# Starting the first block's FFN five slots later in a slot-scheduled attention and FFN kernel

## The chip, the core and the metric

The kernel runs on one core of a Trainium2 chip. The metric is device time in microseconds (us), the median of three runs. One execution is also profiled, and it has a time and a span of its own (first to last instruction).

The engines are named as in the profile: PE (TensorE matmuls; PEld its weight loads), DVE (VectorE), ACT (ScalarE), POOL (GpSimd) and SP (the queue that issues most DMAs). A trailing q (SPq) is an engine's sequencer.

## The reference

```python
# u, v: (4, 3136, 256), z: (4, 3136, 64)
scores = (1.0 / S) * np.matmul(z, z.transpose(0, 2, 1))
attn = np.maximum(scores, 0.0) ** 2
x = u * np.matmul(attn, v)
# w_in (256, 1024), conv_w (3, 1024), w_out (1024, 256)
h = np.maximum(x @ w_in, 0.0)
conv_out = sum(conv_w[k] * hp[:, k:k + S, :] for k in range(3))   # hp: h padded by one row
gate = 1.0 / (1.0 + np.exp(-conv_out))
return h * gate @ w_out
```

This is attention with squared ReLU in place of softmax, multiplied by `u`, and an FFN of 1024 channels whose gate is a three-tap convolution along the sequence. The FFN weights arrive as 64-bit floats.

## The kernel before

**Tiling.** Each batch's 3136 queries are cut into six blocks of 512 and a remainder of 64. There are 24 blocks (`NBLK`). A block goes over 25 key tiles (`NJ`) of 128 keys, one per *slot*, so there are 600 slots, numbered through; block 0 is slots 0 to 24. Products are made accurate by splitting each operand into a high and a low part, so that one product takes two or three matmuls. A slot's attention is eight matmuls of 512 columns: two for scores (`scores`, lines 409 and 410, into a PSUM bank named `s`, for the tile four slots ahead) and six for attention times values (`attend`, line 535, three into the accumulator `av0`, three into `av1`).

**Between scores and attention.** ACT takes the ReLU (line 489, `t<-s`), DVE squares it (line 504, `s<-s,t`), ACT makes the high part (line 513, `ah<-s`), DVE the low part (line 171, `al<-s,ah`). In later blocks some tiles come by a transposing DMA instead and ACT squares them.

**The joint of two blocks.** `av0` and `av1` are single buffers. When a block ends, `gate_x` multiplies its result by `u`: DVE reads `av0` (line 672, `ut<-av,ut`) and ACT reads `av1` (line 667, `x<-av`). Only then may PE write the next block's first product. Once per batch the remainder's product (line 617, 25 matmuls) comes first at the joint, and it writes `av0`.

**The FFN of a block** runs beside the attention of the next. `split_x` (class `xl<-ut,xh`, on DVE and POOL) makes its operands; its hidden channels are eight tiles, `f` 0 to 7. Tile f has six matmuls in (lines 705 to 708), then ACT, DVE (two taps at line 749, a product at line 763) and POOL (`gl<-hb,gh`), and ten and eleven slots later six matmuls out (lines 780 to 782), three in each slot. `FS` gives a tile's slot, counted from the start of the next block.

**The weights** are turned from 64-bit to two 32-bit parts in the kernel, in 16 *pieces* of 128x256, one per `f` for `w_in` and `w_out`. `WS` holds a piece's slot. A piece costs DVE two instructions (lines 316 and 320) in that slot and two (lines 328 and 333) in the next; ACT two, POOL two and ACT a copy. The intermediate values of the first pieces lie in PSUM (tile `wp`), by the limit `W_P = 22` on the slot or by the list `W_B`; those of the others in SBUF (tile `wr`). For the pieces in `W_A`, line 333 is replaced by ACT and POOL work.

**The order** is written out by hand: `at(slot, class, ...)` appends a call to a slot, the loop over `k` emits them class by class, and each engine works its instructions off in that order. In a slot, `PE0` calls (matmuls out) come before `attend`; scores and `PE1` calls (matmuls in) come after it. Below slot `K_O` odd slots' scores go to other PSUM banks than `s`, and ReLU and square are emitted before the splits.

Of the kernel before, what the change touches and what calls it, by code (L numbers as in the profile page):

```python
# [30 lines left out]
DG = [1, 8, 15, 22]  # L31


K_O = 35
Q0 = 3
C0 = [0, 1, 2, 3, 16, 17, 22, 23, 4, 5, 18, 19, 8, 9, 20, 21, 6, 7, 10, 11, 14, 15, 12, 13, 24]

FS = [2, 5, 8, 11, 15, 18, 21, 24]  # L40
RELU, TAP, ST1, ST2, SIG, GATE, GHI, OUT0, OUT1 = 1, 2, 2, 3, 4, 4, 5, 10, 11
EVAC = 12
UL = 18
XS = 1

C_GATE, C_ST1, C_ST2, C_G, C_SIG, C_HI = 0, 2, 2, 2, 1, 3
C_RELU, C_TAP, C_XS, C_EV, C_V = 3, 1, 3, 3, 5
# [2 lines left out]
WARM = 7  # L50
VO = 4
Z1 = -3
WS = [2, 6, 8, 12, 16, 19, 21, 25, 27, 33, 36, 38, 40, 41, 46, 52]
WST = [0, 1, 1, 2, 3]
W_E = ["GGGGGGGGGGGGGGGG", "AAAAAAAAAAAAAAAA"]
W_C = 7
W_A = [9, 14]
W_B = [6, 7]
SQ = [26, 46]
W_P = 22  # L60

# [18 lines left out]
def kernel(  # L80
# [21 lines left out]
    NJ = (S + P - 1) // P  # L102
# [5 lines left out]
    FC = DFF // P  # L108
# [288 lines left out]
    def scores(k):  # L397
# [3 lines left out]

        if k < K_O and k % 2:
            tag, n = ("ph", 2) if k < NJ else (f"o{k // 2 % 2}", 1)
# [415 lines left out]
    V, A, G = nc.vector, nc.scalar, nc.gpsimd  # L819
# [4 lines left out]
    PRE, MID, VEC, POST, PE0, PE1 = range(6)  # L824

    def at(slot, cls, fn, *args):
        ev[slot][cls].append((fn, args))
# [3 lines left out]
    for q in zs[2:]:  # L831
        s = min(C0.index(j) for j in range(q * CB, min(q * CB + CB, NJ))) - LA - 3
# [11 lines left out]
    for b in range(1, B):  # L844
        k0 = (b * QB - 1) * NJ
        for q in range(QB + 1):
            s = k0 - (QB - 2 - q) * NJ + (12 if q % 2 == 0 else 4)
            if q == QB - 2:
                s = k0 + 6
            elif q == QB - 1:  # L850
                s = k0 + NJ + 6
            elif q == QB:
                s = k0 + 9
            if b == 1 and q < 2:
                s = (Q0 - QB) * NJ + NJ + k0 + 4 + 8 * q
# [3 lines left out]
        for j in range(0, NJ, 2):  # L859
            s = k0 + max(last[j] + 2, last.get(j + 1, 0) + 2, V0 + V1 * j // NJ)  # L860
            if j == NJ - 1:
                s = k0 + V0 - 2
# [5 lines left out]
    for blk in range(1, NBLK):  # L868
        s = blk * NJ + E3
# [4 lines left out]
    for blk in range(PK, NBLK):  # L874
        s = blk * NJ + (R_E if blk % QB == RB else E24[blk % QB])
# [6 lines left out]
    for b in range(B):  # L882
# [9 lines left out]
        for i in range(n + 1):  # L892
            s = k5 + (R_J + 2 * i + R_L * (i == n - 1) // 2 if i < n else R_D + 1) + 1
# [14 lines left out]
    def prep_w_at(n, what, f, i, s):  # L908
        if not wps and W_P:
            wps["w"] = ps.tile([P, 2, D], F32, tag="o1", name="wp")  # L910
        bank = wps["w"] if s < W_P else None
        if i in W_B and not n:
            bank = ps.tile([P, 512], F32, tag="ph", name="wp", bufs=2).rearrange("p (a n) -> p a n", a=2)
        prep_w(n, what, f, *(E[x[i]] for x in W_E), bank, nc.gpsimd if i in W_A else None)

    need = [(NJ + FS[f], "in", f) for f in range(FC)] + [(NJ + FS[f] + OUT0, "out", f) for f in range(FC)]
    for i, (_, what, f) in enumerate(sorted(need)):
        s = WS[i]
        at(s - 4, POST, load_w, what, f)
# [2 lines left out]
    for n in range(4):  # L922
        at(W_C + n, POST, prep_conv, n)
    for blk in range(NBLK):
        at(blk * NJ + UL, POST, load_u, blk)

    def before_end(slot, *args):
        if slot < NS:
            at(slot, *args)

    for blk in range(NBLK - 1):
        k0 = (blk + 1) * NJ
        at(k0, C_GATE, gate_x, blk, G)
        at(k0 + XS, C_XS, split_x, blk, (V, G))
        for f in range(FC):
            s = k0 + FS[f]
            if s == NS - 1:
                break
            at(s, POST, ffn_halo, blk, f)
            at(s, PE1, ffn_in, blk, f)  # L940
            at(s + RELU, C_RELU, ffn_relu, blk, f)
            at(s + RELU, C_RELU, ffn_keep, blk, f)
            at(s + TAP, C_TAP, ffn_tap, blk, f)
            at(s + ST1, C_ST1, ffn_conv, blk, f, 1)
            at(s + ST2, C_ST2, ffn_conv, blk, f, 2)
            before_end(s + SIG, C_SIG, ffn_sig, blk, f)
            before_end(s + GATE, C_G, ffn_gate, blk, f, G)
            before_end(s + GHI, C_HI, ffn_hi, blk, f, A)
            before_end(s + GHI, PE1, ffn_lo, blk, f, G)
            before_end(s + OUT0, PE0, ffn_out, blk, f, 0)  # L950
            before_end(s + OUT1, PE0, ffn_out, blk, f, 1)
        if blk < NBLK - 2:
            at(s + EVAC, C_EV, evac, blk)
            at(s + EVAC + 2, POST, store, blk)
# [97 lines left out]
    def run(fns):  # L1052
        for fn, args in fns:
            fn(*args)

    with tc.manual_schedule():
# [15 lines left out]
        for k in range(-LA, NS):  # L1072
            e = ev[k]
            run(e[PRE])
            early = k + LT < K_O
            if early and 0 <= k + LT:
# [81 lines left out]
```

## Time and profile before

| | |
|---|---|
| runs | 1467.34, 1466.86, 1466.7; median 1466.86 us |
| profiled execution | 1467.12 us, of which the span is 1465.3 us |
| busy share of the span | PE 99%, PEld 86%, DVE 78%, ACT 80%, POOL 59% |
| granted TensorE clock | 1.00 of full speed over the span |
| DMA | 205.24 MB, mean 140 GB/s |

Matmul rows overlap: one of 512 columns is 0.38 us long, and in a full stretch the next begins 0.22 us after it. So the busy share of PE says little here; the number of matmuls in a stretch tells how full PE is. DVE's rows overlap in the same way by some 0.08 us.

### The profile page before, as it was taken

To read this page: it belongs to the slowest core of one execution; us is meant where nothing else is said; L and a number is where in the kernel's file an instruction comes from. 1 tells how busy PE (TensorE), PEld (TensorE's weight loads), DVE (VectorE), ACT (ScalarE), POOL (GpSimd) and SP (SyncE) were. 2 spreads that over 40 slices of the span, in tenths; PEclk is the share of its full clock that TensorE was granted. 3 is DMA by queue.
4 is the path that set the end of the run, shared out by engine and by line. 5 is a ranking of instruction groups with operands and counts; after the bars stand their busy time and mean duration, and the time that the engine had idled before them with its cause. 6 is when DMAs were issued, how large, how long until landed. Compare 5 with 4: busy or idle time off the path is not lost.

```text
span 1465.3 us, 22715 instructions
## 1 busy us (share of the span) xinstructions
PE 1451.6 (99%) x6781; PEld 1260.7 (86%) x6781; DVE 1143.4 (78%) x1776; ACT 1178.5 (80%) x2246; POOL 864.0 (59%) x1218
## 2 busy tenths in 40 slices
PE   9999999999999999999999999999999999999998
PEld 7778888888888888888888888888888888888887
DVE  8998777768787777767777877876778777787677
ACT  8878887878877877878888788787887777878767
POOL 7875656447866654545776654554586654554433
PEclk9999999999999999999999999999999999999999
DMA  6544666865445556678444555586644446567621
GB/s 198 164 132 104 153 142 156 169 150 138 147 134 142 135 132 157 138 149 178 133 149 132 138 140 134 140 172 138 157 149 137 132 122 150 129 132 168 133 63 37
DMA packets 432380, 205.24 MB, mean 140 GB/s; under 512 B 330753, under 2 KB 411905, under 8 KB 432257
## 3 DMA queue, kind: packets, MB, share of 16 engines
q1 hardware_dynamic: 431584, 203.40, 56.9%
q8 instruction: 53, 0.87, 0.3%
q14 instruction: 71, 0.57, 0.1%
q10 hardware_dynamic: 672, 0.40, 0.1%
HBM read 36.59 MB, written 86.90 MB: 84 GB/s over the span
## 4 chain that ended last, share of the span: by engine, by line
PE 87%; POOL 4%; ACT 3%; DVE 3%; issue 2%; DMA 0%; SPq 0%; ACTq 0%; POOLq 0%; DVEq 0%
PE av L535 46%; PE ph L708 5%; PE o L780 5%; PE o L782 5%; PE ph L705 5%; PE o L781 5%; PE ph L706 5%; PE s L409 4%; PE s L410 4%; PE av L617 1%; DVE ph L749 1%; POOL vv L171 1%; POOL pl L439 1%; ACT ph L744 1%; DVE al L171 1%
## 5 line engine op out<-in xcount | busy, mean ns | idle before, releaser
L535 PE MATMUL av<-ah,vv 128*128 128x512 f32 x2400 | 708.7, 379 | 1.4 <-ACT ah L513 0.7
L171 DVE TENSOR_TENSOR al<-s,ah 128x512 fp32r<-128x512 f32 x576 | 397.5, 690 | 225.4 <-PE av L535 116.8
L535 PEld LDWEIGHTS av<-ah,vv 128*128 128x128 f32 x2400 | 449.5, 189 | 64.9 <-ACT ah L513 1.1
L535 PE MATMUL av<-al,vv 128*128 128x512 f32 x1152 | 437.0, 379 | 0.4
L171 POOL TENSOR_TENSOR gl<-hb,gh 128x512 fp32r<-128x512 f32 x192 | 245.3, 1277 | 157.1 <-ACT gh L174 149.3
L749 DVE SCALAR_TENSOR_TENSOR ph<-hb,cw,ph 128x512 f32<-128x512 f32 x384 | 286.8, 747 | 9.4 <-ACT ph L744 9.0
L439 POOL COPY pl<-t 128x1024 uint16<-128x1024 uint16 (+1 forms) x257 | 260.9, 1017 | 2.2 <-DMA dq<-pl 1.1
L535 PEld LDWEIGHTS av<-al,vv 128*128 128x128 f32 x1152 | 217.7, 189 | 32.6 <-DVE al L171 1.8
L504 DVE TENSOR_TENSOR s<-s,t 128x512 f32<-128x512 f32 x275 | 191.8, 697 | 61.5 <-ACT t L489 60.8
L489 ACT ACTIVATE t<-s 128x512 f32<-128x512 f32 x277 | 166.1, 599 | 64.1 <-PE s L410 60.0
L513 ACT CAST ah<-s 128x512 fp32r<-128x512 f32 x277 | 163.3, 590 | 59.8 <-DVE s L504 59.5
L756 ACT ACTIVATE ph<-ph 128x512 f32<-128x512 f32 (+1 forms) x200 | 115.4, 577 | 78.1 <-DVE ph L749 74.7
L739 POOL COPY halo<-hb 128x2 f32<-128x2 f32 x160 | 31.1, 194 | 240.6 <-ACT hb L734 232.2
L484 ACT ACTIVATE s<-tp 128x512 f32<-128x512 f32 x278 | 165.3, 596 | 4.9 <-DMA tp<-dd 3.0
L705 PE MATMUL ph<-xh,wih 128*128 128x512 f32 x384 | 145.8, 380 | 1.1 <-DVE hb L763 1.1
L780 PE MATMUL o<-gh,wol 128*128 128x512 f32 x384 | 145.9, 380 | 0.0
L782 PE MATMUL o<-gl,woh 128*128 128x512 f32 x384 | 145.5, 379 | 0.0
L706 PE MATMUL ph<-xh,wil 128*128 128x512 f32 x384 | 145.5, 379 | 0.0
L781 PE MATMUL o<-gh,woh 128*128 128x512 f32 x384 | 145.5, 379 | 0.0
L744 ACT ACTIVATE ph<-hb,cw 128x512 f32<-128x512 f32 x192 | 133.7, 696 | 6.2 <-POOL halo L739 0.4
L763 DVE TENSOR_TENSOR hb<-ph,hb 128x512 f32<-128x512 f32 x192 | 131.8, 686 | 5.1 <-ACT ph L756 0.7
L734 ACT ACTIVATE hb<-ph 128x512 f32<-128x512 f32 x192 | 114.2, 595 | 17.7 <-PE ph L708 16.3
(138 smaller groups left out, 2091.3 us busy)
## 6 DMA issues: line engine op xcount, KB each, us to landing
dq<-pl SPq DMA_DIRECT2D x232, 256.0 KB, 2.7
st<-in_v_dram SPq DMA_DIRECT2D x48, 256.0 KB, 3.1
ut<-in_u_dram SPq DMA_DIRECT2D x24, 512.0 KB, 4.1
out_dram<-ob SPq DMA_DIRECT2D x19, 512.0 KB, 3.8
st<-in_z_dram SPq DMA_DIRECT2D x24, 256.0 KB, 3.2
sh<-sc SPq DMA_DIRECT2D x44, 128.0 KB, 2.4
dd<-pl SPq DMA_DIRECT2D x69, 64.0 KB, 2.2
dd<-pl SPq DMA_DIRECT2D x23, 192.0 KB, 2.4
```

The lines of the kernel that those rows point to most:

```text
L171: eng.tensor_tensor(out=out, in0=a, in1=b.bitcast(F32), op=ALU.subtract)
L439: nc.gpsimd.tensor_copy(pl[k], src.bitcast(U16).rearrange("p (n h) -> p h n", h=2))
L484: nc.scalar.activation(sc[k][:, :NB], tp[k], AF.Square, scale=SC1**-0.5)
L489: nc.scalar.activation(rl[k], sc[k][:, :NB], AF.Relu, scale=SC1)
L504: nc.vector.tensor_tensor(out=s, in0=s, in1=rl[k], op=ALU.mult)
L535: nc.tensor.matmul(o, lhsT=w[:, j, d], rhs=pairs(r), start=first and i == 0, stop=last and i == len(ops) - 1)
L705: nc.tensor.matmul(o, lhsT=wih[:, dc, w], rhs=pairs(xh[blk][:, dc]), start=(dc == 0), stop=False)
L706: nc.tensor.matmul(o, lhsT=wil[:, dc, w], rhs=pairs(xh[blk][:, dc]), start=False, stop=False)
L749: nc.vector.scalar_tensor_tensor(out=c, in0=hb[blk, f][:, k : e + k], scalar=cw[:, f, k : k + 1], in1=c, op0=ALU.mult, op1=ALU.add,)
L780: nc.tensor.matmul(o, lhsT=wol[:, f, d], rhs=pairs(h), start=(f == 0), stop=False)
L781: nc.tensor.matmul(o, lhsT=woh[:, f, d], rhs=pairs(h), start=False, stop=False)
L782: nc.tensor.matmul(o, lhsT=woh[:, f, d], rhs=pairs(l), start=False, stop=(f == FC - 1))
```

## The change

Block 0's FFN is moved by `LAG = 5` slots, block 1's by four, and so on to block 4's by one; from block 5 on nothing moves. The eight tiles of a moved block are three slots apart throughout (`FSL`), so each moved block takes 24 slots and not 25. `split_x`, `evac` (the copy out) and the store move with their block, and `load_u` of blocks 2 to 5 moves where its buffer would not be free. The loop that emits matmuls in and out is otherwise the same.

The sixteen pieces are put at slots 2 to 57 and no longer 2 to 52, three or four apart from slot 10 on, and piece 8 joins the pieces with intermediate values in PSUM. The limit `K_O` moves along by five.

```diff
-K_O = 35
+K_O = 40
 FS = [2, 5, 8, 11, 15, 18, 21, 24]
+FSL = [2, 5, 8, 11, 14, 17, 20, 23]
+LAG = 5
-WS = [2, 6, 8, 12, 16, 19, 21, 25, 27, 33, 36, 38, 40, 41, 46, 52]
+WS = [2, 6, 10, 13, 17, 20, 24, 28, 32, 36, 39, 43, 46, 49, 53, 57]
-W_B = [6, 7]
+W_B = [6, 7, 8]
...
+    def lag(blk):
+        return max(0, LAG - blk)
+
+    def ffn_slots(blk):
+        x = lag(blk)
+        return [(blk + 1) * NJ + x + s for s in (FSL if x else FS)]
...
-        at(blk * NJ + UL, POST, load_u, blk)
+        at(blk * NJ + max(UL, lag(blk - 2) + 15 if blk > 1 else 0), POST, load_u, blk)
...
-        at(k0 + XS, C_XS, split_x, blk, (V, G))
-        for f in range(FC):
-            s = k0 + FS[f]
+        at(k0 + XS + lag(blk), C_XS, split_x, blk, (V, G))
+        for f, s in enumerate(ffn_slots(blk)):
```

Line numbers of the changed kernel are higher by two up to the schedule and by eight in its loop. Three places are shown.

**DVE, slots 40 and 41.** `al` rows are one per slot; `wr` rows are pieces. Before:

```order
L171 TENSOR_TENSOR al<-s,ah 128x512
L504 TENSOR_TENSOR s<-s,t 128x512
L763 TENSOR_TENSOR hb<-ph,hb 128x512
L316 TENSOR_SCALAR wr<-wr 128x256
L320 TENSOR_SCALAR wr<-wr 128x256
L171 TENSOR_TENSOR al<-s,ah 128x512
L504 TENSOR_TENSOR s<-s,t 128x512
L328 SCALAR_TENSOR_TENSOR wr<-wr 128x256
L333 SCALAR_TENSOR_TENSOR wr<-wr 128x256
L316 TENSOR_SCALAR wr<-wr 128x256
L320 TENSOR_SCALAR wr<-wr 128x256
```

Changed, the same engine from slot 40 on:

```order
L173 TENSOR_TENSOR al<-s,ah 128x512
L506 TENSOR_TENSOR s<-s,t 128x512
L751 SCALAR_TENSOR_TENSOR ph<-hb,cw,ph 128x512
L330 SCALAR_TENSOR_TENSOR wr<-wr 128x256
L335 SCALAR_TENSOR_TENSOR wr<-wr 128x256
L173 TENSOR_TENSOR al<-s,ah 128x512
L506 TENSOR_TENSOR s<-s,t 128x512
L751 SCALAR_TENSOR_TENSOR ph<-hb,cw,ph 128x512
L173 TENSOR_TENSOR al<-s,ah 128x512
L506 TENSOR_TENSOR s<-s,t 128x512
L765 TENSOR_TENSOR hb<-ph,hb 128x512
```

Before, slots 40 and 41 hold six instructions of two pieces; changed, slots 40 to 42 hold the last two of one piece.

**PE, the joint at slot 50** (end of block 1's attention, `av` rows; the first `av` rows are slot 49, the last ones slot 50). Before:

```order
L535 MATMUL av_780<-ah,vv 128x512 x2
L535 MATMUL av_780<-al,vv 128x512
L409 MATMUL s<-zq,zh 128x512
L410 MATMUL s<-zq,zl 128x512
L705 MATMUL ph<-xh,wih 128x512
L706 MATMUL ph<-xh,wil 128x512
L705 MATMUL ph<-xh,wih 128x512
L706 MATMUL ph<-xh,wil 128x512
L708 MATMUL ph<-xl,wih 128x512 x2
L780 MATMUL o_1108<-gh,wol 128x512
L781 MATMUL o_1108<-gh,woh 128x512
L782 MATMUL o_1108<-gl,woh 128x512
```

Changed, from the same place to slot 50's attention:

```order
L537 MATMUL av_773<-ah,vv 128x512 x2
L537 MATMUL av_773<-al,vv 128x512
L411 MATMUL s<-zq,zh 128x512
L412 MATMUL s<-zq,zl 128x512
L537 MATMUL av_1467<-ah,vv 128x512 x2
L537 MATMUL av_1467<-al,vv 128x512
```

Eleven matmuls stood between the two blocks' products, and now two do.

**PE, the joint at slot 125** (end of batch 0's attention; `ar` is the remainder's operand, and its product writes the bank that `av_2891` or `av_2874` held). Before:

```order
L535 MATMUL av_2891<-al,vv 128x512
L535 MATMUL av_2892<-ah,vv 128x512 x2
L535 MATMUL av_2892<-al,vv 128x512
L705 MATMUL ph<-xh,wih 128x512
L706 MATMUL ph<-xh,wil 128x512
L705 MATMUL ph<-xh,wih 128x512
L706 MATMUL ph<-xh,wil 128x512
L708 MATMUL ph<-xl,wih 128x512 x2
L780 MATMUL o_3218<-gh,wol 128x512
L781 MATMUL o_3218<-gh,woh 128x512
L782 MATMUL o_3218<-gl,woh 128x512
L617 MATMUL av_3556<-vv,ar 128x512 x25
```

Changed:

```order
L782 MATMUL o_3259<-gh,wol 128x512
L783 MATMUL o_3259<-gh,woh 128x512
L784 MATMUL o_3259<-gl,woh 128x512
L537 MATMUL av_2874<-ah,vv 128x512 x2
L537 MATMUL av_2874<-al,vv 128x512
L537 MATMUL av_2875<-ah,vv 128x512 x2
L537 MATMUL av_2875<-al,vv 128x512
L619 MATMUL av_3543<-vv,ar 128x512 x25
L707 MATMUL ph<-xh,wih 128x512
```

Six matmuls in and three out stood between the last product and the remainder's; now three matmuls out stand ahead of slot 124's attention and the six in behind the remainder.

## Rows read from the trace of the kernel before

**Rows 1.** The page's first part: busy us of each engine (share of span).

```profile
PE 1451.6 (99%) x6781; PEld 1260.7 (86%) x6781; DVE 1143.4 (78%) x1776; ACT 1178.5 (80%) x2246; POOL 864.0 (59%) x1218
```

**Rows 2.** By stretch: length, busy PE, PEld, DVE, ACT, POOL (count); clock; DMA.

```profile
20.00:50.00 30.00, 29.77 (x136) 24.92 (x135) 29.03 (x59) 27.38 (x61) 28.90 (x36) 1.00 0.71 219
50.00:70.00 20.00, 18.55 (x82) 14.49 (x81) 18.80 (x34) 17.65 (x39) 14.69 (x22) 1.00 0.39 109
70.00:110.00 40.00, 37.24 (x165) 29.93 (x164) 37.42 (x63) 31.55 (x65) 31.06 (x42) 1.00 0.48 142
110.00:140.00 30.00, 30.00 (x141) 25.74 (x140) 25.82 (x44) 26.73 (x53) 18.61 (x28) 1.00 0.33 85
140.00:290.00 150.00, 150.00 (x705) 131.36 (x704) 116.23 (x176) 123.77 (x233) 83.50 (x118) 1.00 0.70 155
```

**Rows 3.** Waits of PE, 0 to 200 us: total us, times, longest.

```profile
PE s L409 <- DVE al L171: 2.5, 3, 1.6
...
PE av L535 <- ACT x L667: 0.6, 1, 0.6
PE ph L708 <- POOL xl L171: 0.5, 1, 0.5
```

**Rows 4.** PE's timeline at 89 us: start, length, [idle before, releaser].

```profile
88.82 0.38 PE L535 MATMUL av<-al,vv 128*128 128x512 f32 x1
90.85 0.51 PE L409 MATMUL s<-zq,zh 128*128 128x512 f32 x1 [1.65 <-DVE al L171]
```

**Rows 5.** DVE's groups by form, 10 to 140 us: count, busy, mean ns, idle before.

```profile
L328 DVE SCALAR_TENSOR_TENSOR wr<-wr 128x256 uint32<-128x256 uint32 x8 | 5.4, 671 | 0.0
L316 DVE TENSOR_SCALAR wr<-wr 128x256 uint32<-128x256 uint32 x8 | 4.6, 576 | 0.0
L320 DVE TENSOR_SCALAR wp<-wr 128x256 uint32<-128x256 uint32 x8 | 4.1, 514 | 0.3
L320 DVE TENSOR_SCALAR wr<-wr 128x256 uint32<-128x256 uint32 x8 | 3.9, 492 | 0.0
L333 DVE SCALAR_TENSOR_TENSOR wr<-wr,wp 128x256 f32<-128x256 uint32 x8 | 3.9, 482 | 0.0
L316 DVE TENSOR_SCALAR wp<-wr 128x256 uint32<-128x256 uint32 x8 | 3.8, 472 | 0.0
L328 DVE SCALAR_TENSOR_TENSOR wr<-wr,wp 128x256 uint32<-128x256 uint32 x8 | 3.7, 466 | 0.0
L333 DVE SCALAR_TENSOR_TENSOR wr<-wr 128x256 f32<-128x256 uint32 x6 | 3.5, 581 | 0.0
```

**Rows 6.** DVE's timeline, two pieces at 75 and 81 to 90 us.

```profile
75.00 0.31 DVE L320 TENSOR_SCALAR wr<-wr 128x256 uint32<-128x256 uint32 x1
...
80.53 0.69 DVE L171 TENSOR_TENSOR al<-s,ah 128x512 fp32r<-128x512 f32 x1
81.14 0.69 DVE L504 TENSOR_TENSOR s<-s,t 128x512 f32<-128x512 f32 x1
...
88.15 1.31 DVE L316 TENSOR_SCALAR wr<-wr 128x256 uint32<-128x256 uint32 x1
```

**Rows 7.** PE, ACT and DVE timelines at slot 50's joint.

```profile
116.77 0.38 PE L535 MATMUL av<-al,vv 128*128 128x512 f32 x1
117.25 0.60 ACT L667 ACTIVATE x<-av 128x512 f32<-128x512 f32 x1
118.22 0.68 DVE L672 SCALAR_TENSOR_TENSOR ut<-av,ut 128x512 f32<-128x512 f32 x1
```

**Rows 8.** PE and DVE timelines at slot 125's joint.

```profile
289.75 0.38 PE L410 MATMUL s<-zq,zl 128*128 128x512 f32 x1
291.04 0.38 PE L535 MATMUL av<-al,vv 128*128 128x512 f32 x1
292.30 0.69 DVE L672 SCALAR_TENSOR_TENSOR ut<-av,ut 128x512 f32<-128x512 f32 x1
293.20 5.56 PE L617 MATMUL av<-vv,ar 128*128 128x512 f32 x25
```

More of the change, by code (lines that the diff above doesn't have):

```diff
@@ L914, in prep_w_at @@
         prep_w(n, what, f, *(E[x[i]] for x in W_E), bank, nc.gpsimd if i in W_A else None)
-    need = [(NJ + FS[f], "in", f) for f in range(FC)] + [(NJ + FS[f] + OUT0, "out", f) for f in range(FC)]
+    def lag(blk):
[3 more added lines that the diff above has]
+        return [(blk + 1) * NJ + x + s for s in (FSL if x else FS)]
+    need = [(s + o, w, f) for w, o in (("in", 0), ("out", OUT0)) for f, s in enumerate(ffn_slots(0))]
     for i, (_, what, f) in enumerate(sorted(need)):
```

## The prediction

> **What bounds the kernel now.** I read the page's first part, then the stretches, then PE's waits, then the timelines where PE stands still. PE is busy for 99% of the span [rows 1], so there is little to gain anywhere; the question is where PE is *not* full. Since matmul rows overlap, I count them. From 140 to 290 us there are 705 in 150 us, 0.213 us each, and this I take as a full PE. By it 136 matmuls are worth 28.9 us in the 30 us from 20 to 50, 82 are worth 17.4 in the next 20, 165 are worth 35.1 in the 40 up to 110, and 141 are worth 30.0 in the 30 up to 140 [rows 2]. PE thus loses 1.1, 2.6 and 4.9 us, and then nothing: 8.6 us in all, before 110 us. That is the room that this change works in (0.6% of the span).
>
> In those 90 us DVE is busy for 29.03 + 18.80 + 37.42 = 85.3 us, 95%; where PE is full it is busy for 116.23 of 150, 77% [rows 2]. Most of the named waits of PE there end with DVE's low part (2.5 us) [rows 3], the longest at 88.82, where the next matmul begins only at 90.85 [rows 4]. So DVE limits this part. What it has there and not later are the sixteen weight pieces.
>
> **What a piece costs.** The four DVE instructions of a piece take 0.472 + 0.514 + 0.466 + 0.482 = 1.93 us with intermediates in PSUM, and 0.576 + 0.492 + 0.671 + 0.581 = 2.32 in SBUF [rows 5]. Neighbouring rows overlap: a row of 0.69 is followed after 0.61 [rows 6]. I take off 0.08 four times: 1.6 and 2.0 us.
>
> The SBUF form is dear because it is uneven: line 320 took 0.31 us at 75.00, and line 316, the same kind of instruction, 1.31 at 88.15 [rows 6], against means of 0.49 and 0.58 [rows 5]. The Trainium skill (SBUF — State Buffer, "Who interferes with whom") gives a rule for this: a `tensor_scalar` from SBUF to SBUF takes a port pair that it shares with GpSimd, and whichever comes second waits for the other's whole instruction; the trace agrees in so far as one SBUF form spans 0.31 to 1.31 us. By that rule a piece that meets no POOL instruction would cost about 1.25 us (0.31 + 0.31 + 0.47 + 0.48 less the overlap) and the balance below would have room; I stay with the mean, since POOL is busy there.
>
> **The spacing, before and changed.** How much DVE has to spare: in FFN blocks 23% of PE's time [rows 2]. A block has 25 x 8 + 8 x 12 = 296 matmuls, 63 us, so a slot lasts 2.5 us and leaves DVE 0.57. In block 0 a slot is eight matmuls, 1.7 us, and DVE has two instructions of 0.61 there [rows 6], so 0.5 is left.
>
> Before, slots 33 to 41 hold five pieces: 10 us against 9 x 0.57 = 5.1. The deficit of 4.9 is just what PE loses from 70 to 110 us. Slots 12 to 27 hold six pieces, 9.6, and the joint's gate and low part of x, 1.2 more, against 16 x 0.5 = 8; the deficit of 2.8 stands beside 2.6 measured from 50 to 70. So the sum of DVE's work explains both.
>
> Changed, slots 13 to 31 hold five pieces, 8.0, and 1.2 for the joint and x, against 19 x 0.5 = 9.5: no deficit. Slots 32 to 58 hold the last eight, one of them now in PSUM: 1.6 + 7 x 2.0 = 15.6 against 27 x 0.57 = 15.4: balanced. Losses are then due to unevenness alone. The bounds: 0, as from 110 to 140 us, where two pieces lie in 30 us [rows 2], and what is lost now. The even spacing puts me near the lower bound, but the balance has nothing to spare: I take 0.3 of 1.1, 1.1 of 2.6 (0.5 of it the wait for POOL's `xl` [rows 3], which moves along with `split_x`, one slot ahead of the matmuls as before), and 1.2 of 4.9. **The stretch gives back 0.8 + 1.5 + 3.7 = 6.0 us**, between 1 and 8.6.
>
> **What the change adds: joints without cover.** The moved matmuls stood between two blocks' products, where PE may not write an accumulator before it has been read. At slot 50 the last product begins at 116.77. ACT reads `av1` from 117.25 to 117.85 and DVE reads `av0` from 118.22 to 118.90 [rows 7]. Eleven matmuls hid all of this. Now only two are left: PE would be ready at 116.77 + 3 x 0.215 = 117.4, waits 0.45 for `av1`, does three matmuls (to 118.5), and waits another 0.4 for `av0`. In the changed order DVE has lines 318 and 322 of a piece just ahead of the gate, ACT one more copy. Free of POOL they cost 0.6 together, held up as at 88.15 two us; against that, DVE is less behind. I take 0.8 (0.4 to 2.0).
>
> At slot 125 the remainder's product waits for `av0`. From the end of the scores at 289.75 + 0.38 = 290.13, ReLU, square and a tap run before DVE's gate, which ends at 292.99; the product begins at 293.20 [rows 8], so the nine matmuls of cover were just enough. In the changed order six matmuls of attention and three of out follow those scores, 1.94 us from 289.97, so PE is ready at 291.9 and waits until 293.1. I take 1.2; the bounds are 0.4 (the gate straight behind the last `av0` matmul) and 1.9 (ready at 291.26, as after 291.04 here).
>
> At slot 100 the six matmuls in go from between the products too, but three out remain ahead of `av1` and three more ahead of `av0`: 0.3 (0 to 0.5). At slots 75 and 150 both kinds still stand there: nothing. **The joints cost 2.3 us**, between 0.8 and 4.4. Behind PE's waiting matmul stand only PE's own; the other engines catch up meanwhile, which I count at nothing.
>
> **Costed at nothing.** The same 6781 matmuls run, so PE's own work is unchanged. Blocks 1 to 5 take their FFN in 24 slots and not 25: DVE's share rises from 77% to some 80%, under the 95% at which PE lost time. Weights are ready three slots or more ahead of use. The copy out keeps its distance to the next block's matmuls out. `K_O` only keeps the extra banks until the FFN needs them. On SP, `load_u` now follows the store of the same buffer by three slots and not five, some 7 us; a wait there would hold up the transposing loads behind it, which are issued ten slots ahead.
>
> **Sum.** 2.3 - 6.0 = -3.7. The profiled execution's 1467.12 becomes 1463.4; it lies 0.26 above the median of 1466.86, so the median becomes **1463.2 us**.
>
> **Rivals.**
> *POOL holds up the pieces.* The seven SBUF pieces now run among the FFN's POOL work. Each has two instructions of lines 316 and 320; 1.31 - 0.31 more for one of them alone is 7 us of DVE more, on a balance without spare. For it: POOL is busy for 74.7 of the 90 us up to 110 [rows 2]. Against it: the means of rows 5 contain this already, and eight such pieces ran before. Then the stretch gives 2.5, the joints take 2.3: 1466.7. The rule above is the page's statement of this mechanism.
>
> *The joints cost little.* If DVE and ACT, no longer behind, read the accumulators at once, the joints take 0.8 and the stretch gives the same 6.0 or a little more: 1461.5. For it: in block 0's joint PE waited only 0.6 for ACT [rows 3] with DVE behind. Against it: the chain of rows 8 hangs on the scores, not on a backlog.
>
> *Slower: the joints decide.* At their upper end they take 4.4, and if the piece ahead of the gate at slot 50 makes its backlog last for several slots, as the one at 88.15 did (2 us), some 6.4 while the stretch gives 2.5: 1470.8. It decides as soon as the joints cost over 3 us more than the stretch gives. Against it: block 1's joint is the only one with a piece at it.
>
> **Chances.** Forecast 0.50, own range 1461.5 to 1465; POOL 0.22; cheap joints 0.21; slower 0.07. About 0.2% (2.9 us) can be told from no change, so faster means under 1463.9. Of the forecast some 0.36 lies there, and all of the cheap joints: 0.57. The same: 0.14 of the forecast and the 0.22 of POOL, 0.36. Slower: 0.07. The range reaches from the cheap joints' far side to just past the POOL case: 1460.0 to 1467.3.
>
> **What would show it.** Right: from 20 to 110 us some 405 matmuls (379 before), DVE still over 90% busy; no wait over 0.8 us on DVE's low part; the remainder's product at slot 125 idle before for about 1.2 us, released by line 674 of DVE; a wait of 0.5 to 1 us before slot 50's product. Wrong: DVE's lines 318 and 322 with means over 0.8 us and PE short up to 130 us (POOL); waits under 0.3 us at both joints; or a gap somewhere after 150 us, where I expect nothing.

## The result: slower, and outside the range

The changed kernel takes 1485.32 us (median of 4 runs, 1483.55 to 1485.83) where the kernel before took 1467.1 beside it: a ratio of 1.0122, 95% interval 1.0106 to 1.0138. Its profiled execution took 1485.49 us, 18.4 more than the one before, with a span of 1483.7.

The stretches of the changed kernel, answering to [rows 2] (length, then busy time and count of PE, PEld, DVE, ACT, POOL, then the granted clock as a share of 2.4 GHz, DMA share, GB/s):

```profile
20.00:50.00 30.00, 29.76 (x132) 24.04 (x131) 27.63 (x55) 26.33 (x59) 27.50 (x34) 1.00 0.67 209
50.00:70.00 20.00, 18.10 (x81) 14.35 (x80) 17.51 (x32) 16.26 (x35) 13.45 (x16) 1.00 0.38 115
70.00:110.00 40.00, 36.61 (x159) 30.40 (x157) 36.43 (x59) 30.86 (x62) 27.25 (x41) 0.96 0.49 143
110.00:140.00 30.00, 25.97 (x110) 21.28 (x110) 23.10 (x39) 22.15 (x45) 15.04 (x22) 0.94 0.23 66
140.00:290.00 150.00, 146.01 (x671) 126.08 (x671) 112.26 (x173) 118.82 (x224) 85.83 (x121) 0.99 0.63 147
```

The first 90 us in a single window, where no matmul that straddles an edge is counted twice:

```profile
20.00:110.00 90.00, 84.47 (x369) 68.78 (x367) 81.57 (x144) 73.45 (x155) 68.19 (x89) 0.98 0.53 159
```

From 20 to 110 us there are 369 matmuls, where there were 379 and I wanted 405: 2.1 us lost in place of a gain. From 110 to 140 there are 110 instead of 141, and from 140 to 290 there are 671 instead of 705: at 0.213 us, 6.6 and 7.2 us lost where nothing was lost before. Most of the loss thus lies where I expected no change.

PE's waits in the changed kernel over the whole span, answering to [rows 3] (us in total, times, longest):

```profile
PE s L411 <- DVE al L173: 4.9, 7, 2.0
PE ph L707 <- ACT dg L385: 3.2, 2, 1.7
PE ph L707 <- ACT sc L553: 2.2, 2, 1.9
PE av L537 <- ACT x L669: 1.9, 2, 1.5
...
PE ph L707 <- ACT rj L599: 1.4, 1, 1.4
```

DVE's low part is waited for 4.9 us instead of 2.7 (2.5 of it in [rows 3]), ACT's `x` 1.9 instead of 0.6 (the joint at slot 25, where a piece now begins at slot 24, and the one at slot 50). New is line 707, the FFN's first matmul in: it waits 6.8 us in all for ACT to read `dg`, `sc` or `rj` out of a PSUM tile `ph`. One of these waits, at slot 47, in the timeline (start, us, engine, line):

```profile
111.52 0.28 PE L380 MATMUL ph<-zq,zl 128*128 128x256 f32 x1
...
112.11 0.58 ACT L758 ACTIVATE ph<-ph 128x512 f32<-128x512 f32 x1
...
112.61 0.59 ACT L491 ACTIVATE t<-s 128x512 f32<-128x512 f32 x1
...
113.08 0.39 ACT L385 ACTIVATE dg<-ph 128x256 f32<-128x256 f32 x1
...
113.53 0.79 PE L707 MATMUL ph<-xh,wih 128*128 128x512 f32 x1 [1.73 <-ACT dg L385]
```

The far scores of the next block (line 380, `ring_score`) have just been written into one of the two `ph` banks. The FFN's tile needs a bank in the same slot. One bank is held by the tile before it, whose DVE product is still to come; so PE waits until ACT, which has lines 758 and 491 ahead of line 385 in its own order, has emptied the other. I call this a collision. Before, the other users of `ph` (`ring_score`, `early`, `rem_scores`) stand one slot behind a tile's, `rem_scores` two. With the tiles five, four, three slots later, four of them fall into a tile's slot: 47, 56, 113 and 122.

The joints at slots 50 and 125, answering to [rows 7] and [rows 8]:

```profile
120.97 0.72 DVE L318 TENSOR_SCALAR wr<-wr 128x256 uint32<-128x256 uint32 x1
120.97 0.38 PE L412 MATMUL s<-zq,zl 128*128 128x512 f32 x1
...
121.51 1.31 POOL L173 TENSOR_TENSOR gl<-hb,gh 128x512 fp32r<-128x512 f32 x1
...
121.61 1.36 DVE L322 TENSOR_SCALAR wr<-wr 128x256 uint32<-128x256 uint32 x1
...
122.89 0.68 DVE L674 SCALAR_TENSOR_TENSOR ut<-av,ut 128x512 f32<-128x512 f32 x1
...
123.63 0.48 PE L537 MATMUL av<-ah,vv 128*128 128x512 f32 x1 [1.04 <-DVE ut L674]
...
309.29 0.92 PE L619 MATMUL av<-vv,ar 128*128 128x512 f32 x3 [0.86 <-DVE ut L674]
```

At slot 50 the piece's line 322 runs beside POOL's `gl` for 1.36 us, just ahead of the gate (line 674) that PE waits for. At slot 125 PE waits 0.86 us.

Behind some gaps PE also runs at half clock. The stretches around one, after the matmul at 140.25, from which to the next PE lost 2.1 us:

```profile
143.00:144.00 1.00, 1.00 (x7) 0.84 (x6) 0.79 (x3) 0.00 (x0) 0.10 (x1) 0.97 0.00 0
144.00:147.00 3.00, 3.00 (x9) 2.37 (x8) 0.00 (x0) 1.67 (x3) 2.04 (x3) 0.50 0.68 153
148.00:150.00 2.00, 2.00 (x11) 1.73 (x11) 1.70 (x3) 1.77 (x5) 0.00 (x0) 1.00 0.88 194
```

Nine matmuls in 3 us at 1.2 GHz. Three such places make up the 0.96, the 0.94 and the 0.99 of the first table: 0.04 x 40 + 0.06 x 30 + 0.01 x 150 = some 4.9 us of full clock that was not granted in this execution. How much of it the time contains is not shown: of the four executions the two whose mean clocks lie furthest apart, 0.996 and 0.999, took 1485.49 and 1485.15 us.

### The profile page after: what moved, and what is told of

Its sections match the earlier page's. It is cut to its first block, busy times and chain, and to the rows that moved or that the text cites. A ratio compares the mean times of both kernels' runs of the same rounds, so it can differ in the third digit from the quotient of the medians.

```text
span 1483.7 us, 22700 instructions
## 1 busy us (share of the span) xinstructions
PE 1458.9 (98%) x6781; PEld 1264.9 (85%) x6781; DVE 1145.1 (77%) x1776; ACT 1180.1 (80%) x2246; POOL 863.8 (58%) x1218
## 4 chain that ended last, share of the span: by engine, by line
PE 87%; ACT 5%; DVE 4%; issue 2%; POOL 1%; DMA 0%; SPq 0%; ACTq 0%; DVEq 0%; POOLq 0%
PE av L537 46%; PE ph L707 5%; PE ph L710 5%; PE ph L708 5%; PE o L782 5%; PE o L784 5%; PE o L783 5%; PE s L411 4%; PE s L412 4%; PE av L619 1%; DVE ph L751 1%; DVE al L173 1%; ACT ph L746 1%; ACT t L491 1%; ACT hb L736 1%
```

## The experiments

Each ratio is against runs of the kernel before on the same chip. The times of different experiments are often from different chips, so they are compared by these ratios, at 1467 us; a difference of two ratios is good to some 2 to 3 us. What PE loses at a place is the distance from one matmul's start to the next beyond the first one's own 0.216 us (0.108 where it has half the columns). In kernels derived from the changed one, line numbers are two higher than in the kernel before (707 for 705).

### Collisions and joints, taken away from the changed kernel

**e1_banks**: the other users of `ph` moved by a slot or two, off the tiles' slots.

```
-        s = blk * NJ + E3
+        s = blk * NJ + E3 + {2: 1, 4: -1, 5: 1}.get(blk, 0)
...
```

In the part left out, the slot of `early` changes by -2, -1 and -1 for blocks 2, 4 and 5, and that of `rem_scores` by one in the first batch.

> The changed kernel with the other users of the two banks `ph` moved off the FFN's tiles: the diagonal scores of blocks 2 and 5 one slot later, of block 4 one earlier, the early scores of blocks 2, 4 and 5 one or two earlier, the remainder's scores of batch 0 one later. Theory banks: the new waits of PE's line 707 on ACT (dg 3.2, sc 2.2, rj 1.4, in all 6.8 us) go, and with the two at 111.5 and 140.3 us the half clock behind them, 1.8 us each: 1485.3 - 6.8 - 3.6 = 1475, range 1473 to 1479. Rival joints and DVE: the time is lost between the blocks and to DVE, PE is late anyway and meets these waits elsewhere: 1482 to 1486.

Measured: 1480.81, ratio 1.0082 (1.0067 to 1.0097), between the two theories. No wait for `dg`, `sc` or `rj` is left, but this one doubled (from 4.9):

```profile
PE s L411 <- DVE al L173: 9.9, 9, 2.8
```

So the collisions are real, but near where two of them had stood PE now waits for DVE: 1.9 us are lost at 111.5 and 3.0 at 145.6. One reason may be that a stop of PE had given DVE time to catch up. Another is in the rows: ahead of the stop at 145.6 the piece's line 335 takes 1.48 us beside POOL's `sh<-sc,sh`, which adds up the `early` scores that this edit moved. By the ratios 0.0040 x 1467 = 5.9 us came back, not the full loss.

**e2_joints**: the scores and the matmuls queued behind them go ahead of the product at slots 50 and 100; at slot 125 the queued matmuls alone.

```
-            if rem or k == NJ:
+            fed = k in (NJ, 2 * NJ, 4 * NJ)
+            if rem or fed:
+                if k == RB * NJ:
+                    run(e[PE1])
+                    e[PE1].clear()
...
```

> The changed kernel with cover at three joints: scores and matmuls in ahead of the products in slots 50 and 100, the matmuls in ahead of the remainder's product in slot 125. Theory joints as forecast: the waits there go, 1.7 us at slot 50, 1.0 at 125: 1485.3 - 2.7 = 1482.6. Theory banks: the same, for this is the smaller part. Rival (the joints start the loss, everything later follows from their delay and the clock): 1474 to 1478.

Measured: 1489.16, 1.0139 (1.0114 to 1.0165): no gain is shown. The four executions lie between 1484.26 and 1493.83 us, at mean clocks from 0.999 to 0.994, so the median alone would not settle 2.7 us. In the profiled one, the fastest, the joints' waits at slots 50 and 125 are gone, but at slot 50 PE loses 3.0 us on DVE's low part instead. PE's stops at 82, 111 and 140 us are as long as in the changed kernel, and yet the clock holds:

```profile
70.00:110.00 40.00, 35.70 (x160) 29.31 (x159) 36.39 (x60) 31.26 (x63) 27.83 (x41) 1.00 0.50 146
110.00:140.00 30.00, 24.35 (x111) 20.45 (x111) 23.19 (x39) 21.91 (x46) 15.16 (x22) 1.00 0.24 66
140.00:290.00 150.00, 145.04 (x675) 125.64 (x674) 113.46 (x172) 119.84 (x226) 85.78 (x122) 1.00 0.65 148
```

**e3_both**: the two edits together.

> Both of the former edits. If waits add up: 1485.3 - 10.4 - 2.7 = 1472, which leaves the waits on DVE and on ACT before 110 us and the fall of the clock at 86 us. If one cause stands behind both, the better of the two alone, some 1475 to 1482.

Measured: 1482.43, 1.0092 (1.0077 to 1.0107). Beside e1_banks no gain is shown here either: at slot 50 PE loses 1.9 us on DVE's low part. DVE is behind, whoever waits for it first.

### The pieces alone, the lag alone

**e4_pieces**: the kernel before with evenly spaced pieces, nothing else.

```
-WS = [2, 6, 8, 12, 16, 19, 21, 25, 27, 33, 36, 38, 40, 41, 46, 52]
+WS = [2, 6, 10, 13, 17, 20, 24, 27, 30, 33, 36, 39, 42, 45, 48, 52]
```

> The kernel before with evenly spaced pieces alone: slots 2, 6, 10, 13, 17, 20, 24, 27, 30, 33, 36, 39, 42, 45, 48, 52, no FFN moved. Theory of the forecast (clusters of pieces cost 6 us before 110 us, spacing gives most of it back): 1467.1 - 4 = 1463, range 1461 to 1465. Rival (DVE's whole work limits the stretch, or pieces among the FFN's POOL and ACT work are held up wherever they stand): 1466 to 1469.

Measured: 1473.97, 1.0036 (1.0021 to 1.005): slower. This is the part from which I had expected 6 us. Its longest wait:

```profile
73.80 0.38 PE L535 MATMUL av<-al,vv 128*128 128x512 f32 x1
76.16 0.49 PE L409 MATMUL s<-zq,zh 128*128 128x512 f32 x1 [1.99 <-DVE al L171]
```

**e5_lag**: the changed kernel with the old `WS` and `W_B`.

> The changed kernel with the list of weight pieces of the kernel before (and the PSUM form for pieces 6 and 7 alone, as there): the later FFN is the only part of the change left. Theory A, the parts of the loss add up: spacing the pieces evenly alone cost 5.2 us on the kernel before, so taking it back here gives 1480 us (1478 to 1482), and the waits on DVE's low part go, while those of the first FFN matmul for a bank (slots 47, 56, 113, 122) and of the joints stay. Theory B, the phase of a piece against the FFN tiles decides: the old pieces were in step with the old tile slots, and with the tiles five slots later only two of the seven from slot 33 on still are, so the waits on DVE's low part stay: 1483 to 1487. Theory C, the pieces are the whole loss and the later FFN is harmless: 1466 to 1470.

Measured: 1482.39, 1.0096 (1.0082 to 1.011). Theory C falls; by the time A and B both come close. The waits speak against A, by which those on DVE's low part would go, since they grow from 4.9 to 7.0:

```profile
PE s L411 <- DVE al L173: 7.0, 8, 2.4
```

Those for `dg`, `sc` and `rj` are the same to the digit as in the changed kernel.

**e8_lagbanks**: e5_lag with the edit of e1_banks.

> The changed kernel with the old list of pieces, as in e5_lag, and with the other users of the two banks moved out of the tiles' slots, as in e1_banks. Left of the change are the later FFN and its joints. Theory A, additive: e1_banks less 5.2 us, 1475 to 1477 us, of which 3 to 4 are the joints at slots 50 and 125 and the rest waits on DVE's low part. Theory B, phase: 1479 to 1483, with waits on DVE's low part of over 1 us at slots 33 to 48. If the later FFN costs nothing but its collisions: 1467 to 1470.

Measured: 1473.94, 1.0038 (1.0024 to 1.0052). Beside e5_lag on the same chip this is the price of the four collisions with the old pieces: **8.5 us**. The waits that go are 3.2 + 2.2 + 1.4 = 6.8; so does a stretch at half clock from 113 to 117 us, in which 1.7 us of full clock were not granted; DVE's low part is waited for 0.5 more. The total is below what either theory had said; of the lag without collisions 5.6 us are left.

What these are is only in part a matter of pieces held up. The means of the four SBUF forms sum to 2.15 us here, less than the 2.32 of [rows 5]. Ahead of the longest stop, 2.5 us from 80.86 on, no row of a piece is long; DVE itself waits twice for ACT, whose rows follow each other without a pause:

```profile
80.26 0.74 DVE L751 SCALAR_TENSOR_TENSOR ph<-hb,cw,ph 128x512 f32<-128x512 f32 x1
...
81.51 0.42 DVE L330 SCALAR_TENSOR_TENSOR wr<-wr 128x256 uint32<-128x256 uint32 x1 [0.51 <-ACT wr L327]
...
82.85 0.69 DVE L173 TENSOR_TENSOR al<-s,ah 128x512 fp32r<-128x512 f32 x1 [0.59 <-ACT ah L511]
...
83.60 0.50 PE L411 MATMUL s<-zq,zh 128*128 128x512 f32 x1 [2.35 <-DVE al L173]
```

**e6_one**: the kernel before with a single collision, at slot 196.

```
-        s = blk * NJ + E3
+        s = blk * NJ + E3 - (blk == 8)
```

> The kernel before with one edit: the far scores of the eighth block boundary (slot 197) are computed one slot earlier, in an FFN tile's own slot (196), some 480 us into the span where PE is full. This measures one PSUM collision by itself. Theory A: the FFN matmul behind them has to wait for ACT's evacuation one slot later, one gap on PE of 1.5 to 2.1 us, released by ACT's `rj` or `sc`: the time grows by 1.5 to 2 us (1468.4 to 1469 where the kernel before has 1467), and by 3 to 4 us if the granted clock falls behind it as it did in the changed kernel. Theory B, where PE has slack behind it the gap is made up: no more than 0.5 us.

Measured: 1469.12 beside 1467.85, 1.0007 (0.9998 to 1.0016). The timeline shows it:

```profile
469.43 0.28 PE L378 MATMUL ph<-zq,zl 128*128 128x256 f32 x1
...
470.19 0.39 ACT L383 ACTIVATE dg<-ph 128x256 f32<-128x256 f32 x1
...
470.63 0.48 PE L705 MATMUL ph<-xh,wih 128*128 128x512 f32 x1 [0.93 <-ACT dg L383]
```

Here ACT read `dg` 0.76 us after line 378 began, and PE lost 1.1 us, with the clock at 1.00 throughout; at slot 47 of the changed kernel ACT came to it 1.56 us after, since it had still been waiting for DVE, and PE lost 1.9. The median's difference of 1.3 agrees, just under theory A's 1.5, though its interval reaches just below nothing.

### The phase of the pieces

A piece is called in step when its slot is also that of an FFN tile. The ramp is the ten slots between a block's first matmuls in and its first matmuls out.

**e7_phase**: the kernel before with the pieces from 33 on one slot later, at 34, 37, 39, 41, 42, 47, 53. The piece at 27, which the expectation counts among the moved ones, stays there.

> The kernel before with the last eight weight pieces (from slot 27 on) each one slot later (28, 34, 37, 39, 41, 42, 47, 53), so that those that stood in an FFN tile's slot now stand in the slot behind it; their distances from each other are unchanged from slot 34 on. Theory B, the phase against the tiles decides: new waits on DVE's low part of 1 to 2 us at two or more of these pieces, 1470 to 1474 us where the kernel before has 1467. Rival, only the distances between pieces count (my reckoning in the prediction): the old wait at slot 39 stands a slot later and nothing else changes, 1466 to 1468.

Measured: 1470.81, 1.0019 (1.0011 to 1.0028). Slower by 3 us, at the lower edge of theory B; four waits on DVE's low part cost 0.8 to 1.8 us each where one of 1.8 had stood.

**e9_p0** and **e11_p2**: e8_lagbanks with the last eight pieces at 28, 32, 35, 38, 41, 44, 47, 53 (in step with the tiles but for the first), or all eight two slots later.

> The later FFN with the two banks kept free (as in e8_lagbanks, 1473.9 us); the first eight pieces as before the change, the last eight at 28, 32, 35, 38, 41, 44, 47, 53, each but the first in the slot of an FFN tile. Theory B, the phase of a piece against the tiles decides: the waits on DVE's low part go but for 1 to 2 us, 1468 to 1470. Theory R, the ramp decides: in the ten slots between a block's first matmuls in and its first matmuls out (32 to 41 here, 27 to 36 in the kernel before) PE has 8 + 6 x 8 / 25 = 9.9 matmuls per slot, 2.1 us, and DVE still its 77% of 2.5 = 1.9, so it has only 2 us to spare in all ten, about one piece. Four pieces stand there here (32, 35, 38, 41), so PE still loses 4 to 6 us there: 1472 to 1474, and within 1.5 us of e11_p2.

> As e9_p0, with the last eight pieces two slots later (30, 34, 37, 40, 43, 46, 49, 55), out of step with the tiles, at the same distances. Theory B, phase: waits of 1.5 to 2.5 us at four or more of the pieces, 1474 to 1477, over 4 us above e9_p0. Theory R, the ramp: three or four pieces in it as in e9_p0, 1471 to 1474, within 1.5 us of e9_p0.

Measured: 1470.13, 1.002 (1.0011 to 1.0029), and 1476.47, 1.0067 (1.0053 to 1.0081). The same work at the same distances, 6.3 us apart on one chip: between these two the phase decides, and not the ramp, which would have left them within 1.5 us. Part of the reason can be seen in the pieces' rows on DVE. In step (duration min/median/max in ns):

```profile
L318 DVE TENSOR_SCALAR wr<-wr x8: 325/760/1206, 62.2 to 124.0; 128x256 uint32<-128x256 uint32 x8
L322 DVE TENSOR_SCALAR wr<-wr x8: 284/330/1176, 62.5 to 124.2; 128x256 uint32<-128x256 uint32 x8
L330 DVE SCALAR_TENSOR_TENSOR wr<-wr x8: 400/480/949, 64.8 to 126.4; 128x256 uint32<-128x256 uint32 x8
L335 DVE SCALAR_TENSOR_TENSOR wr<-wr x6: 409/486/499, 65.1 to 126.8; 128x256 f32<-128x256 uint32 x6
```

and out of step:

```profile
L318 DVE TENSOR_SCALAR wr<-wr x8: 310/335/936, 65.5 to 134.7; 128x256 uint32<-128x256 uint32 x8
L322 DVE TENSOR_SCALAR wr<-wr x8: 293/600/1379, 65.7 to 135.0; 128x256 uint32<-128x256 uint32 x8
L330 DVE SCALAR_TENSOR_TENSOR wr<-wr x8: 411/867/1446, 68.0 to 139.1; 128x256 uint32<-128x256 uint32 x8
L335 DVE SCALAR_TENSOR_TENSOR wr<-wr x6: 411/530/1256, 69.3 to 140.5; 128x256 f32<-128x256 uint32 x6
```

What these 30 instructions take beyond 0.5 us each sums to 4.4 us in step and 7.5 out of step, half of the 6.3. Of the rest 1.3 us are a single stop, at 69.05, before DVE's low part of x: there the piece at slot 30 runs into `split_x` at slot 31. In step too PE still loses 1.9 us, at 81.54; as in e8_lagbanks, DVE's low part there comes behind ACT's `ah`. One place of e11_p2 in the timeline:

```profile
89.45 1.03 POOL L441 COPY pl<-t 128x1024 uint16<-128x1024 uint16 x1
...
89.70 0.93 DVE L318 TENSOR_SCALAR wr<-wr 128x256 uint32<-128x256 uint32 x1
...
90.44 1.30 POOL L173 TENSOR_TENSOR gl<-hb,gh 128x512 fp32r<-128x512 f32 x1
90.55 1.38 DVE L322 TENSOR_SCALAR wr<-wr 128x256 uint32<-128x256 uint32 x1
...
91.85 0.67 DVE L173 TENSOR_TENSOR al<-s,ah 128x512 fp32r<-128x512 f32 x1
...
92.58 0.50 PE L411 MATMUL s<-zq,zh 128*128 128x512 f32 x1 [2.41 <-DVE al L173]
```

Line 318 ends within 0.2 us of POOL's copy `pl`, line 322 within 0.2 us of POOL's `gl`, and only then comes the low part for which PE waits 2.4 us. The Trainium skill (SBUF — State Buffer, "Who interferes with whom") says that `tensor_scalar` can run in a mode that takes the port pair which DVE shares with GpSimd, and that the second to come is then blocked for the whole of the other's instruction; these rows, 0.93 and 1.38 us where the shortest take 0.31 and 0.29, agree.

**e12_step**: the kernel before with pieces 38 and 41 moved to 30 and 43. **e13_ramp**: e8_lagbanks with the ramp nearly empty and most pieces out of step, [2, 6, 8, 12, 16, 19, 21, 25, 27, 29, 36, 42, 45, 48, 51, 54].

> The kernel before with two pieces moved: from slots 38 and 41 to 30 and 43, so that all from 27 on stand in an FFN tile's slot (27, 30, 33, 36, 40, 43, 46, 52) and no two are nearer than three slots. Theory B, phase (and my prediction's own reckoning of DVE's balance): the wait of 1.8 us at 88.8 us goes, 1464 to 1466 where the kernel before has 1467. Theory R: the ramp, slots 27 to 36, has four pieces and not three, so a wait of about 2 us comes up at slots 31 to 36 in exchange, as in e4_pieces at 73.8 us: 1467 to 1469.

> As e8_lagbanks, with the ramp (slots 32 to 41) all but empty of pieces: two go ahead of it (27, 29), one stays in it (36), and five follow once the matmuls out have begun (42, 45, 48, 51, 54), each of them a slot behind a tile's, out of step. Theory R: the waits of 2.5 and 2.2 us at slots 38 and 41 go, and nothing over 1 us comes in their place: 1467 to 1469.5, 4 to 6 us below e8_lagbanks. Theory B, phase: six of these pieces are out of step, 1473 to 1477.

Measured: 1466.88, 0.9999 (0.999 to 1.0008), and 1477.37, 1.0065 (1.0053 to 1.0078). e13_ramp refutes the ramp as the sole cause: emptier, and by the ratios 4 us slower than e8_lagbanks. (Two of its stops, 1.6 us at `split_x`'s `xl` and 2.2 at slot 50's joint, stand behind the pieces of slots 29 and 48.) e12_step lost the wait at 88.8 and got one of the same 1.8 us at 71.4, which the ramp theory had said; phase is thus not the whole rule.

### Is it POOL?

**e11_p2_nopl** and **e9_p0_nopl**: 22 of POOL's copies left out; an older copy (`kept`) is stored in their place.

```
+        if 28 <= k <= 58 and kept:
+            pl[k] = kept[-1][:, :, :n]
+            return
         pl[k] = wk.tile(...)
...
```

> e11_p2 (pieces two slots behind the tiles, 1476.5 us) with POOL's 22 copies of score rows (`pl`, about 1.04 us each) left out in slots 28 to 58; an older copy is stored in their place, so those rows of the far scores are not computed, and everything else runs as before. Theory P, POOL holds the pieces up: the rows of the SBUF pieces on DVE of over 0.8 us (ten in e11_p2) fall to three or fewer, and the time to 1470 to 1472. Theory C, the chain of DVE and ACT is short of time in the tile-free slots whatever POOL does: the waits of 2.6 us at slot 41 and 2.2 us at slot 47 stay, 1474.5 to 1477.

> e9_p0 (pieces in step, 1470.1 us) with the same 22 copies on POOL left out in slots 28 to 58. Theory P: its pieces are held up too (eight rows of over 0.8 us), so 1468 to 1469.5, and within 1.5 us of e11_p2_nopl, since no phase is then better than another. Theory C: 1469.5 to 1470.5, and 4 us or more below e11_p2_nopl.

Measured: 1471.74, 1.0032 (1.0019 to 1.0045), and 1468.03, 1.0002 (0.9993 to 1.0011). The pieces of e11_p2_nopl:

```profile
L318 DVE TENSOR_SCALAR wr<-wr x8: 309/330/1250, 65.7 to 130.3; 128x256 uint32<-128x256 uint32 x8
L322 DVE TENSOR_SCALAR wr<-wr x8: 292/341/1411, 65.9 to 130.5; 128x256 uint32<-128x256 uint32 x8
L330 DVE SCALAR_TENSOR_TENSOR wr<-wr x8: 457/478/1371, 68.2 to 134.7; 128x256 uint32<-128x256 uint32 x8
```

The medians fall to 0.33, 0.34 and 0.48, the rows over 0.8 us from eleven to four (theory P had said three or fewer), and the time, by the ratios, by 5.1 us (2.6 in step). That is what leaving out POOL's copies is worth out of step. But the two phases still differ by 3.7 us, which theory P had not allowed. The four long rows left each stand beside another of POOL's (`gl` three times, `xl` once), and the time beyond 0.5 us is still 3.5 against 1.9. PE's two stops that have no match in step stand behind such rows: 1.1 us at 69.25 for DVE's low part of x, behind line 330, which takes 1.37 us beside POOL's `xl`, and 2.1 us at 89.74 for DVE's low part, behind line 318, which takes 1.22 us beside `gl`. Of the two waits that theory C wanted to stay, the one of 2.6 us is this last one, and the one of 2.2 is gone. Whether POOL is the whole remainder, or DVE's chain has a part in it, I did not separate.

**e14_best**: the kernel before with the tail 27, 33, 36, 40, 43, 46, 49, 52. **e16_fed**: e9_p0 with the joint edit of e2_joints.

> The kernel before with the pieces from slot 27 on at 27, 33, 36, 40, 43, 46, 49, 52: all in a tile's slot as in e12_step, but 30 is empty again (where e12_step had a new wait of 1.8 us at slot 31 or 32) and 49 is filled. Theory: the waits of 1.8 us at 88.8 us (before) and at 71.4 us (e12_step) are both gone, 1464.5 to 1466. Rival: the three pieces from slot 43 to 49 bring a wait of their own at 108 to 120 us, 1466.5 to 1468.

> e9_p0 (the later FFN, banks free, pieces in step, 1470.1 us) with the scores put ahead of the product at slots 50, 100 and 125, as in e2_joints. Theory: of what is left of the loss, 2.8 us, the joints at slots 50 and 125 are 1.3 (waits of 0.5 and 0.8 us); these go, 1468.5 to 1469.5. Rival, as in e2_joints: a wait on DVE's low part takes the place of the one at slot 50, 1470 to 1472.

Measured: 1466.24, 0.9993 (0.9985 to 1.0002): the 1.8 us waits at 88.8 us (before) and at 71.4 (e12_step) are both gone, and the interval just includes no change. And 1471.06, 1.0022 (1.0013 to 1.0031): the wait at slot 125 is gone, at slot 50 PE loses 1.7 us on DVE's low part instead of 0.5, and nothing is gained.

## Why the prediction was wrong

The change can be built up from the ratios, at 1467 us: the later FFN with free banks and pieces in step costs 2.9 us (e9_p0); with the old pieces, most of which the lag puts out of step, 5.6 (e8_lagbanks); with the collisions 14.1 (e5_lag); with the new pieces 17.9. In this order the four terms are 2.9, 2.7, 8.5 and 3.8. Each is good to some 2 to 3 us, so the second and the last are hardly clear of nothing. In another order, with the new pieces, the collisions come out at 5.9 (e1_banks). That is within the noise of 8.5, but the waits show why it can be less: 6.8 us for ACT went and 5.0 for DVE's low part came, against 0.5 with the old pieces.

- **"Costed at nothing" failed most: 8.5 us.** I counted that "the same 6781 matmuls run" and looked at DVE's share and at when weights are ready, but not at the buffers the moved matmuls write. `ph` has two banks and, beside the few pieces in `W_B`, four kinds of user, and the old tile slots had left the one slot behind each tile free for the others. The trace could not show a wait that wasn't there; the tables of slots (FS, FSL, E3, E24, R_D) could: 25 + 22 = 47 is 30 + 17. The warning sign that I named, a gap after 150 us, came true: PE lost 1.6 us each at 280.0 and 300.9.
- **"The stretch gives back 6.0 us" has the wrong sign.** Even spacing alone, a little tighter than in the change, costs 5.3 us (e4_pieces). The sum of DVE's work fitted the loss before, but that was luck as far as the runs show: by the same sum e12_step was to take 1464 to 1466, and it took 1466.88. (That sum was also a little off: the piece at slot 27 is an SBUF piece, so the six of slots 12 to 27 come to 10.0 us and not 9.6.) The loss comes in single stops, six of 0.8 to 2.1 us in e4_pieces, and not as a deficit over many slots. Nor has a piece a fixed price: its instructions take 0.3 to 0.5 us free of POOL and up to 1.45 beside it. The means of the four SBUF forms, 2.32 us in [rows 5], sum to 2.63 in e4_pieces and 2.73 in e11_p2, so that my reason against the POOL rival, that the means "contain this already", failed there. But this is not all of it. In the changed kernel the sum is 2.47, some 1 us more for its seven pieces, and the sign that I had named for POOL, lines 318 and 322 with means over 0.8 us, did not come (0.70 and 0.58). In e8_lagbanks the pieces are cheaper than before and PE still stops for 2.5 us behind ACT and DVE. How much of the step's failure is POOL's and how much the chain's stays open.
- **The joints** came out near their terms: 0.48 + 1.21 = 1.7 us at slot 50 (0.8 taken, 0.4 to 2.0 given), and the held-up line 322 ahead of the gate was the case named; 1.0 at slot 125 (1.2 taken). I had missed the joint at slot 25, where the piece now at slot 24 makes PE lose 1.7 us instead of 0.8 for ACT's `x`; so block 1's joint was not the only one with a piece at it. Removing the joints at slots 50 to 125 showed no gain, though (e2_joints, e3_both, e16_fed).
- **The slower rival** had 1470.8 and a deciding mechanism at slot 50; that one alone was not what decided. The clock, of which some 4.9 us were not granted in the profiled execution, was in no term.

## What to carry to other kernels

Before moving instructions by whole slots, list every tile they write, how many buffers it has, and in which slot each user takes and frees one: a shared pair of PSUM banks can turn a move that adds no work into stops of PE. The price of a DVE instruction between SBUF tiles depended here on what POOL did at that moment, so a mean taken at the old places need not hold at new ones; look for its minimum and maximum and ask which of the two the new place will give. Ask also what the waiting engine's own chain (here ACT, DVE, PE) has to spare in that slot, since a piece that nothing holds up can still come at the wrong time. And where one engine is late in many places, a wait removed elsewhere can come back at that engine, as in e1_banks, e2_joints and e16_fed.

## What the hardware showed

After stops of PE of 2.1, 1.9 and 2.1 us (at 82, 111 and 140 us) the granted clock fell to half for about 3 us, some two to four us after the stop's beginning; the stop of 1.8 us at 88.8 in the kernel before did not do it [rows 2, 4]. The size of one stop does not decide it: e8_lagbanks lost 2.5 and 2.2 us in single stops and shows 1.00 in all stretches around them, and e2_joints, with the same three stops as the changed kernel and one of 3.0 us at 119, shows 1.00 from 70 to 290 us. What does decide it no run here shows. An evacuation by ACT costs PE more than its own 0.39 us: 1.1 us in a quiet place, 1.9 where ACT was itself behind.
